# Moving work off ScalarE in an S5-scan and GeGLU kernel: one scaling for both parts of C, slab 3 normalised on VectorE, y of slab 1 a gate step later

## The chip, the cores and the metric

One core of a Trainium2 chip. The time is the device time of one execution in microseconds (us). Each kernel is timed in several executions beside executions of the kernel before on the same chip; one of them is profiled. The page of a profile gives the span, which is the time from the first to the last recorded instruction; executions take 2.1 to 3.3 us longer than their span. Engines: PE is TensorE (PEld its weight loads), ACT is ScalarE, DVE is VectorE, POOL is GpSimd, SP is SyncE, which issues most DMAs here. All executions told of were in the fast state.

## The reference

```python
xn = layernorm(x)                                   # x: 2048 tokens x 512
h[t] = Lam_bar * h[t-1] + xn[t] @ B_bar.T           # complex state, 512 wide
s = 2 * Re(h @ C.T) + xn * Dskip
g = silu((gelu(xn @ w_gate) * (xn @ w_up)) @ w_down)   # 512 -> 1376 -> 512
out = x + s * g
```

## The kernel before

Tokens are cut into four slabs (0 to 3) of 512. For each slab PE runs eleven gate steps (a gate and an up product of four matmuls each), the products u for the scan, and the down product f. The scan itself is on DVE: rotate (`pp`, `qq`, `Wt`), four scans (`Ft`), rotate back to `hst`. The output product y of a slab is put between the gate steps of the next one: eight matmuls add onto a seed (`z`, the skip term) that ACT has copied into the PSUM bank.

```python
U_BUFS = 3
Z_BUFS = 9
U0_AT = (5, 7)
Y_AT = {1: (9, 10, 11, 11), 2: (5, 6, 7, 8), 3: (2, 4, 6, 8)}   # gate steps that hold y of the slab before
XN_AT = {1: 1, 2: 3}                                            # gate steps that scale the slab after
...
def ffn(s, j, at):            # one gate step: PE products, two ACT evictions, every second step a DVE product
    g_ps, u_ps = gu_mm(s, j, 0), gu_mm(s, j, 1)
    ...
    ACT(out=gt[:fs, i, :], in_=g_ps[:fs, :], func=AF.Gelu_apprx_tanh)
    ACT(out=ub[:fs, i, :], in_=u_ps[:fs, :], func=AF.Copy)
    ...
    if j == NFT - 1:          # the last product, 96 rows
        dve(now() + lag, 0.36, lambda: TT(out=at[:fs, j, :], in0=gt[:fs, 0, :], in1=ub[:fs, 0, :], op=ALU.mult))
...
def y_seed(s, m):
    y_ps = psum.tile([P, D], FP32, name="y_ps", tag="ps")
    ACT(out=y_ps[:, :], in_=zs[s, m], func=AF.Copy)
...
def ln_out(s, m):             # xn = x * rstd - mean * rstd
    ACT(out=xn[:], in_=x_tok[:, s * M + m, :], func=AF.Identity, scale=rs[:, s, m : m + 1], bias=nb[:, s, m : m + 1])
    xn_out(s, m, xn)          # SP: DMA transpose of xn into xnT
...
            if s == 1:        # after slab 1's u products
                for m in (M - 2, M - 1):
                    epi(0, m, y_mm(0, m, hsts[0], y_pss[0, m]), g2s[0, m])   # ends in an output DMA on SP
            if s == 1:
                load_x(3)     # SP: x of slab 3
            for m in range(M):
                g2s[s, m] = down(s, m, ats[s])
                if s == 1:
                    ln_act(3, m)   # ACT: sums for the statistics of slab 3
```

`dve(ready, cost, f, late)` first lets older waiting DVE work out of a list as far as its estimated end allows, then emits `f`: the order on DVE is fixed when the kernel is built, by estimates. On the chip DVE keeps it: where it waits (0.66 us for y in a timeline below), the work behind waits too.

Of the kernel before, what the change touches and what calls it, by code (L numbers as in the profile page):

```python
# [10 lines left out]
AF = mybir.ActivationFunctionType  # L11
ALU = mybir.AluOpType
FP32 = mybir.dt.float32
# [6 lines left out]
def kernel(  # L20
# [17 lines left out]
    nc = tc.nc  # L38
    P = 128
    S = 2048  # L40
    D = 512
# [5 lines left out]
    NS = S // TS  # L47
    M = TS // P
    NFT = (F + P - 1) // P
# [7 lines left out]
    TSC = nc.vector.tensor_scalar  # L57
    STT = nc.vector.scalar_tensor_tensor
    ACT = nc.scalar.activation
# [5 lines left out]
    work = ctx.enter_context(tc.tile_pool(name="work", bufs=2))  # L65
# [5 lines left out]
    x_tok = consts.tile([P, NS * M, D], BF16, name="x_tok")  # L71
# [5 lines left out]
    C2 = consts.tile([P, 2, NPT, D], BF16, name="C2")  # L77
# [4 lines left out]
    CT = work.tile([P, 2, NPT, D], BF16, name="CT", tag="hst")  # L82
# [31 lines left out]
    for h in range(2):  # L114
        for ri, src in enumerate((A_B_re, A_B_im)):
            for pt in (h * H2, h * H2 + 1):
                nc.sync.dma_start_transpose(
                    out=BT[:, ri, :, pt * P : (pt + 1) * P], in_=src[pt * P : (pt + 1) * P, :]
# [27 lines left out]
    def small(name, w=NPT):  # L146
        return consts.tile([P, w], FP32, name=name)
# [9 lines left out]
    rs = consts.tile([P, NS, M], FP32, name="rs")  # L157

    def bn(s, m):
        nc.vector.bn_stats(out=st[:, s, m, :], in_=x_tok[:, s * M + m, :])  # L160
# [134 lines left out]
    cre, cim, ncre = small("cre"), small("cim"), small("ncre")  # L295
# [25 lines left out]
        GS(out=ncre[:], in0=cre[:], scalar1=-1.0, scalar2=None, op0=ALU.mult)  # L321

    def fold_c(pt):
        tA = work.tile([P, D], FP32, name="tA", tag="tt", bufs=3)
        tB = work.tile([P, D], FP32, name="tB", tag="tt", bufs=3)
        ACT(out=tA[:], in_=CT[:, 1, pt, :], func=AF.Copy, scale=cim[:, pt : pt + 1])
        ACT(out=tB[:], in_=CT[:, 0, pt, :], func=AF.Copy, scale=cim[:, pt : pt + 1])
        dve(now() + 0.8, 0.66, lambda: STT(
            out=C2[:, 0, pt, :], in0=CT[:, 0, pt, :], scalar=cre[:, pt : pt + 1], in1=tA[:],
            op0=ALU.mult, op1=ALU.subtract,  # L330
        ))
        dve(now() + 1.6, 0.66, lambda: STT(
            out=C2[:, 1, pt, :], in0=CT[:, 1, pt, :], scalar=ncre[:, pt : pt + 1], in1=tB[:],
            op0=ALU.mult, op1=ALU.subtract,
        ))

# [5 lines left out]
    def now():  # L342
        return clk["pe"]
# [9 lines left out]
    def flush(key):  # L353
        while any(w[3] == key for w in waiting):
            pop()

    def drain(t, late):
        while waiting and max(clk["dve"], waiting[0][0]) + waiting[0][1] <= t + late:
            pop()

    def dve(ready, cost, f, late=0.8):
        drain(ready, late)
        clk["dve"] = max(clk["dve"], ready) + cost
        f()

    def later(ready, cost, f, key=None):
        waiting.append((ready, cost, f, key))
# [1 line left out]

    ini = {}  # L370
    U_BUFS = 3
    Z_BUFS = 9
    U0_AT = (5, 7)
    Y_AT = {1: (9, 10, 11, 11), 2: (5, 6, 7, 8), 3: (2, 4, 6, 8)}
    XN_AT = {1: 1, 2: 3}

    def u_pair(s, h):
        cols = slice(s * TS, (s + 1) * TS)
# [126 lines left out]
# [3 lines that stand above are left out]
        y_pss[s, m] = y_ps  # L508
# [45 lines left out]
    nb = consts.tile([P, NS, M], FP32, name="nb")  # L554
    nm = consts.tile([P, NS, M], FP32, name="nm")
# [6 lines left out]
    def ln_small(s):  # L562
        total, var = sx[:, s, 0, :], sx[:, s, 1, :]

        def f():
            STT(out=mq[:, s, :], in0=total, scalar=-1.0 / (D * D), in1=total, op0=ALU.mult, op1=ALU.mult)
            TSC(out=nm[:, s, :], in0=total, scalar1=-1.0 / D, scalar2=None, op0=ALU.mult)
            STT(out=var, in0=var, scalar=1.0 / D, in1=mq[:, s, :], op0=ALU.mult, op1=ALU.add)
            TSC(out=var, in0=var, scalar1=EPS, scalar2=None, op0=ALU.add)

        dve(now() + 1.0, 0.3, f)
        nc.gpsimd.tensor_tensor(out=rs[:, s, :], in0=var, in1=mhalf[:], op=ALU.pow)
        nc.gpsimd.tensor_tensor(out=nb[:, s, :], in0=nm[:, s, :], in1=rs[:, s, :], op=ALU.mult)


    zs, y_pss = {}, {}
# [1 line left out]
    def skip(s, m, xn):  # L578
        if s == 0:

            z = x_tok[:, (NS - 1) * M + m, :]
        else:
            z = work.tile([P, D], BF16, name="z", tag="z", bufs=Z_BUFS)[:]
        zs[s, m] = z
        later(0.0, 0.36, lambda: TT(out=z, in0=xn[:], in1=Db[:], op=ALU.mult), ("z", s, m))

    def ln_out(s, m):
        flush(("z", s - 1, m))
        xn = work.tile([P, D], BF16, name="xn", tag="xn", bufs=4)
        ACT(out=xn[:], in_=x_tok[:, s * M + m, :], func=AF.Identity, scale=rs[:, s, m : m + 1], bias=nb[:, s, m : m + 1])  # L590
        xn_out(s, m, xn)

    def xn_out(s, m, xn):
        c0 = s * TS + m * P
        nc.sync.dma_start_transpose(out=xnT[:, :, c0 : c0 + P], in_=xn[:])
        if s > 1:
            skip(s, m, xn)


# [14 lines left out]
    def ln_vector_small(x):  # L614
        G.tensor_scalar(out=vx[:, x, :], in0=mv[:, x, :, 1], scalar1=EPS, scalar2=None, op0=ALU.add)
        G.tensor_tensor(out=rs[:, x, :], in0=vx[:, x, :], in1=mhalf[:], op=ALU.pow)
        G.tensor_tensor(out=nb[:, x, :], in0=mv[:, x, :, 0], in1=rs[:, x, :], op=ALU.mult)
        G.tensor_scalar(out=nb[:, x, :], in0=nb[:, x, :], scalar1=-1.0, scalar2=None, op0=ALU.mult)
# [9 lines left out]
    later(11.2, 1.25, lambda: TT(out=v5(t1_[:]), in0=sa, in1=cB, op=ALU.mult))  # L628
    later(11.2, 1.25, lambda: TT(out=v5(t2_[:]), in0=ca, in1=sB, op=ALU.mult))
    later(11.2, 1.25, lambda: TT(out=sin_b[:], in0=t1_[:], in1=t2_[:], op=ALU.add))  # L630
    xs1 = {}

    def norm1(m):
        xs1[m] = norm0(m, 1)

    for s in range(NS):
        for j in range(NFT):
            if s > 0 and j in Y_AT[s]:
                y_seed(s - 1, Y_AT[s].index(j))
            ffn(s, j, ats[s])  # L640
            if s == 0:
                if j == 1:
                    coefficients()
                if j == NFT - 1:
                    flush("n")
                    ln_vector_small(2)
                if j == 8:
                    coefficients_end()
                if j == 2:
                    flush("n1")  # L650
                    ln_vector_small(1)
                    rs1_at = clk["dve"] + 2.4
                if j == 3:
                    for m in range(M):
                        flush(("z", 0, m))
                        dve(max(rs1_at, 0.0), 0.36, lambda m=m: norm1(m), 0.4)
                        xn_out(1, m, xs1[m])
                if j in U0_AT:
                    chain(0, U0_AT.index(j), u_pair(0, U0_AT.index(j)), hst0)
                if j == 5:  # L660
                    for m in range(M):
                        later(0.0, 0.72, lambda m=m: (bn(2, m), bn_end(2, m)), "n")
                    for m in range(M):
                        skip(1, m, xs1[m])
                    nc.sync.dma_start(
                        out=wd[:, 0 : NFT - 1, :],
                        in_=B_w_down[0 : (NFT - 1) * P, :].rearrange("(k p) d -> p k d", p=P),
                    )
                    nc.sync.dma_start(out=wd[:FL, NFT - 1, :], in_=B_w_down[(NFT - 1) * P : F, :])
                    load_c()  # L670
            else:
                if j in Y_AT[s]:
                    m = Y_AT[s].index(j)
                    epi(s - 1, m, y_mm(s - 1, m, hsts[s - 1], y_pss[s - 1, m]), g2s[s - 1, m])
                if s < NS - 1 and XN_AT[s] <= j < XN_AT[s] + M:
                    ln_out(s + 1, j - XN_AT[s])
        if s < NS - 1:
            hsts[s + 1] = work.tile([P, 2, NPT, TS], BF16, name="hst", tag="hst")
            ats[s + 1] = work.tile([P, NFT, TS], BF16, name="at", tag="at")
            for h in range(2):  # L680
                chain(s + 1, h, u_pair(s + 1, h), hsts[s + 1])
                if s == 1:
                    y_seed(0, M - 2 + h)
            if s == 1:
                for m in (M - 2, M - 1):
                    epi(0, m, y_mm(0, m, hsts[0], y_pss[0, m]), g2s[0, m])
            if s == 1:
                load_x(3)
            for m in range(M):
                g2s[s, m] = down(s, m, ats[s])  # L690
                if s == 0:
                    fold_c(m)
                if s == 1:
                    ln_act(3, m)
            if s == 1:
                ln_small(3)
    s = NS - 1
# [41 lines left out]
```

## Time and profile before

| | before |
|---|---|
| time, median of the first 3 executions | 184.47 us |
| span of the profiled execution | 181.3 us |
| busy: PE, DVE, ACT | 175.1, 160.5, 116.0 us |
| idle time of PE in the middle of the run | 0.96 us, once |

### The profile page before, as it was taken

The page shows a single profiled execution, that of the slowest core. Times are in us where ns is not written, and L with a number is a line of the kernel's source. Part 1 is how long each engine was busy: PE and PEld are TensorE (multiplying, and loading weights), DVE is VectorE, ACT ScalarE, POOL GpSimd, SP SyncE. Part 2 cuts the span into 40 slices and gives each one's busy share as a digit, 9 for nine tenths or more (in the row PEclk, how much of TensorE's full clock was granted, in tenths as well). Part 3 has the DMA queues.
Part 4 walks back from the last instruction along what each step waited for, and adds up shares of the span by engine and source line. Part 5 has one row for each costly group of instructions (what it writes and reads, how often), then busy time and mean ns, then how long its engine had stood idle before and what let it go on. Part 6 is the DMA issues. An engine that isn't in the chain of part 4 may idle for free.

```text
span 181.3 us, 2449 instructions
## 1 busy us (share of the span) xinstructions
PE 175.1 (97%) x858; PEld 82.8 (46%) x858; DVE 160.5 (89%) x252; ACT 116.0 (64%) x206; POOL 21.5 (12%) x50
## 2 busy tenths in 40 slices
PE   7899999999999999999999799999999999999992
PEld 2684444444444444444444344444444444444451
DVE  3889999998978999999969999999999899996063
ACT  3599667777799982781599974467429545574500
POOL 3794416004000000000004000000000000000000
PEclk9999999999999999999999999999999999999999
DMA  5999497950002300002300223100000000000011
GB/s 154 312 337 185 95 240 224 255 90 9 0 0 50 66 4 29 29 0 68 106 4 0 42 58 74 36 29 0 0 0 0 29 5 29 29 29 0 0 55 61
DMA packets 25643, 12.37 MB, mean 68 GB/s; under 512 B 15808, under 2 KB 25632, under 8 KB 25632
## 3 DMA queue, kind: packets, MB, share of 16 engines
q1 hardware_dynamic: 25456, 12.16, 27.6%
q8 instruction: 6, 0.10, 0.2%
q10 hardware_dynamic: 176, 0.07, 0.1%
q14 instruction: 5, 0.04, 0.1%
HBM read 6.46 MB, written 2.10 MB: 47 GB/s over the span
## 4 chain that ended last, share of the span: by engine, by line
PE 64%; DVE 17%; ACT 12%; DMA 3%; issue 2%; SPq 0%; DVEq 0%; ACTq 0%
PE f_ps L495 16%; PE up_ps L243 13%; PE g_ps L243 13%; PE u_ps L387 11%; PE y_ps L515 11%; DVE Ft L434 4%; DMA x_tok<-in_A_x_dram 3%; ACT gt L479 3%; ACT ub L480 2%; ACT junk L560 2%; DVE pp L404 2%; DVE qq L404 2%; DVE yg L528 2%; DVE hst L408 1%; ACT L479 1%
## 5 line engine op out<-in xcount | busy, mean ns | idle before, releaser
L243 PE MATMUL g_ps<-xnT,wg 128*128 128x512 bf16 (+3 forms) x200 | 45.9, 353 | 0.3 <-DVE xnT L203 0.2
L243 PE MATMUL up_ps<-xnT,wu 128*128 128x512 bf16 (+3 forms) x192 | 45.7, 361 | 0.0
L495 PE MATMUL f_ps<-wd,at 128*128 128x512 bf16 (+1 forms) x176 | 38.7, 379 | 0.0
L479 ACT ACTIVATE gt<-g_ps 128x512 bf16<-128x512 f32 (+1 forms) x44 | 27.0, 614 | 16.4 <-PE g_ps L243 16.3
L480 ACT ACTIVATE ub<-up_ps 128x512 bf16<-128x512 f32 (+1 forms) x44 | 27.1, 616 | 5.7 <-PE up_ps L243 5.5
L434 DVE TENSOR_TENSOR_SCAN Ft<-rho,it,Wt 128x512 bf16<-128x512 f32 x24 | 29.3, 1268 | 0.0
L515 PE MATMUL y_ps<-C,hst 128*128 128x512 bf16 x120 | 27.9, 379 | 1.0 <-ACT y_ps L507 1.0
L387 PE MATMUL u_ps<-xnT,BT 128*128 128x512 bf16 x128 | 28.4, 379 | 0.0
L243 PEld LDWEIGHTS <-wg 128*128 128x128 bf16 (+1 forms) x200 | 19.1, 100 | 19.5 <-issue 0.5
L243 PEld LDWEIGHTS <-wu 128*128 128x128 bf16 (+1 forms) x192 | 18.8, 100 | 19.2
L495 PEld LDWEIGHTS <-at 128*128 128x128 bf16 (+1 forms) x176 | 17.2, 98 | 20.8
L392 ACT ACTIVATE U<-u_ps 128x512 bf16<-128x512 f32 x32 | 19.1, 597 | 9.8 <-PE u_ps L387 9.7
L500 ACT ACTIVATE g<-f_ps 128x512 f32<-128x512 f32 x16 | 9.5, 593 | 16.2 <-PE f_ps L495 16.2
L387 PEld LDWEIGHTS <-BT 128*128 128x128 bf16 x128 | 12.5, 98 | 15.0
L515 PEld LDWEIGHTS <-hst 128*128 128x128 bf16 x120 | 11.7, 98 | 15.3 <-issue 1.2
L528 DVE TENSOR_TENSOR yg<-y_ps,g 128x512 bf16<-128x512 f32 x15 | 10.3, 685 | 8.1 <-PE y_ps L515 8.1
L488 DVE TENSOR_TENSOR at<-gt,ub 128x1024 bf16<-128x1024 bf16 x20 | 13.6, 680 | 0.5 <-ACT ub L480 0.4
L408 DVE TENSOR_TENSOR hst<-pp,qq 128x1024 bf16<-128x1024 bf16 x16 | 10.6, 689 | 0.3
L408 DVE TENSOR_TENSOR Wt<-pp,qq 128x1024 bf16<-128x1024 bf16 x16 | 10.4, 688 | 0.2
L404 DVE TENSOR_TENSOR pp<-U,cos_b 128x2048 bf16<-128x2048 bf16 x8 | 9.7, 1218 | 0.1
L404 DVE TENSOR_TENSOR pp<-Ft,cos_b 128x2048 bf16<-128x2048 bf16 x8 | 9.8, 1219 | 0.0
L404 DVE TENSOR_TENSOR qq<-Ft,sin_b 128x2048 bf16<-128x2048 bf16 x8 | 9.8, 1219 | 0.0
(108 smaller groups left out, 146.9 us busy)
## 6 DMA issues: line engine op xcount, KB each, us to landing
out_dram<-ot SPq DMA_DIRECT2D x15, 128.0 KB, 1.7
x_tok<-in_A_x_dram SPq DMA_DIRECT2D x3, 512.0 KB, 6.7
wd<-in_B_w_down_dram SPq DMA_DIRECT2D x1, 1280.0 KB
wg<-in_B_w_gate_dram SPq DMA_DIRECT2D x2, 256.0 KB, 3.7
wu<-in_B_w_up_dram SPq DMA_DIRECT2D x2, 256.0 KB
wg<-in_B_w_gate_dram SPq DMA_DIRECT2D x1, 512.0 KB, 6.5
wu<-in_B_w_up_dram SPq DMA_DIRECT2D x1, 512.0 KB
wg<-in_B_w_gate_dram SPq DMA_DIRECT2D x1, 352.0 KB
```

The costliest lines, as they stand in the source:

```text
L243: nc.tensor.matmul(ps[:fs, a:b], lhsT=w[:, kt, fsl], rhs=xnT[:, kt, s * TS + a : s * TS + b], start=(kt == 0), stop=(kt == KT - 1),)
L387: nc.tensor.matmul(u_ps[:, :], lhsT=BT[:, ri, kt, pt * P : (pt + 1) * P], rhs=xnT[:, kt, cols], start=(kt == 0), stop=(kt == KT - 1),)
L392: ACT(out=U[:, ri, q, :], in_=u_ps[:, :], func=AF.Copy)
L404: TT(out=box[key][:], in0=src()[:], in1=tab[:, hs, :].unsqueeze(1).to_broadcast(W), op=ALU.mult)
L408: return lambda: TT(out=dst()[i], in0=box["pp"][:, i, :, :], in1=box["qq"][:, 1 - i, :, :], op=op)
L434: nc.vector.tensor_tensor_scan(out=box["F"][:, ri, q, :], data0=rho[:, pt : pt + 1].to_broadcast([P, TS]), data1=box["W"][:, ri, q, :], in ...
L479: ACT(out=gt[:fs, i, :], in_=g_ps[:fs, :], func=AF.Gelu_apprx_tanh)
L480: ACT(out=ub[:fs, i, :], in_=u_ps[:fs, :], func=AF.Copy)
L488: dve(now() + lag, 0.63, lambda: TT(out=at[:, j - 1 : j + 1, :], in0=gt[:], in1=ub[:], op=ALU.mult))
L495: nc.tensor.matmul(f_ps[:, :], lhsT=at[:fs, k, m0 : m0 + P], rhs=wd[:fs, k, :], start=(k == 0), stop=(k == NFT - 1))
L515: nc.tensor.matmul(y_ps[:, :], lhsT=hst[:, j // NPT, j % NPT, m0 : m0 + P], rhs=C2[:, j // NPT, j % NPT, :], start=False, stop=(j == 2 * N ...
L528: TT(out=yg[:], in0=y_ps[:, :], in1=g2[:], op=ALU.mult)
```

## The change

Its intent is to take ACT out of PE's way: fewer instructions on ACT (four of the eight scalings of C and the four xn of slab 3 go), and y of slab 1 one gate step later, to give its seed time.

```diff
     def fold_c(pt):
-        tA = ...; tB = ...                            # two tiles, 3 buffers of 512
-        ACT(out=tA[:], in_=CT[:, 1, pt, :], func=AF.Copy, scale=cim[:, pt : pt + 1])
-        ACT(out=tB[:], in_=CT[:, 0, pt, :], func=AF.Copy, scale=cim[:, pt : pt + 1])
+        tc_ = ...                                     # one tile, 2 buffers of 1024
+        ACT(out=tc_[:], in_=CT[:, :, pt, :], func=AF.Copy, scale=cim[:, pt : pt + 1])
...
-    Z_BUFS = 9
+    Z_BUFS = 8
-    Y_AT = {..., 2: (5, 6, 7, 8), ...}
-    XN_AT = {1: 1, 2: 3}
+    Y_AT = {..., 2: (6, 7, 8, 9), ...}
+    XN_AT = {1: 1, 2: 6}
...
     def ln_out(s, m):
+        if s == NS - 1:
+            dve(now() + 0.5, 0.36, lambda: TSC(
+                out=xn[:], in0=x_tok[:, s * M + m, :], scalar1=nm[:, s, m : m + 1], scalar2=rs[:, s, m : m + 1],
+                op0=ALU.add, op1=ALU.mult,
+            ))
+            xs3[m] = xn
+        else:
             ACT(...)                                  # as before, slab 2 only
...
+                if s == 2 and j in (XN_AT[2], XN_AT[2] + 1):
+                    for m in (2 * (j - XN_AT[2]), 2 * (j - XN_AT[2]) + 1):
+                        ln_out(3, m)                  # two xn in each of two steps
+                if s == 2 and j == NFT - 1:
+                    for m in range(M): skip(3, m, xs3[m])
```

(Cut: one small POOL product that the new form of xn doesn't need, and the loop of the old form.)

More of the change, by code (lines that the diff above doesn't have):

```diff
@@ L323, in fold_c @@
     def fold_c(pt):
-        tA = work.tile([P, D], FP32, name="tA", tag="tt", bufs=3)
-        tB = work.tile([P, D], FP32, name="tB", tag="tt", bufs=3)
-        ACT(out=tA[:], in_=CT[:, 1, pt, :], func=AF.Copy, scale=cim[:, pt : pt + 1])
-        ACT(out=tB[:], in_=CT[:, 0, pt, :], func=AF.Copy, scale=cim[:, pt : pt + 1])
+        tc_ = work.tile([P, 2, D], FP32, name="tc_", tag="tt", bufs=2)
+        ACT(out=tc_[:], in_=CT[:, :, pt, :], func=AF.Copy, scale=cim[:, pt : pt + 1])
         dve(now() + 0.8, 0.66, lambda: STT(
-            out=C2[:, 0, pt, :], in0=CT[:, 0, pt, :], scalar=cre[:, pt : pt + 1], in1=tA[:],
+            out=C2[:, 0, pt, :], in0=CT[:, 0, pt, :], scalar=cre[:, pt : pt + 1], in1=tc_[:, 1, :],
             op0=ALU.mult, op1=ALU.subtract,
@@ L332, in fold_c @@
         dve(now() + 1.6, 0.66, lambda: STT(
-            out=C2[:, 1, pt, :], in0=CT[:, 1, pt, :], scalar=ncre[:, pt : pt + 1], in1=tB[:],
+            out=C2[:, 1, pt, :], in0=CT[:, 1, pt, :], scalar=ncre[:, pt : pt + 1], in1=tc_[:, 0, :],
             op0=ALU.mult, op1=ALU.subtract,
@@ L371 @@
     U_BUFS = 3
-    Z_BUFS = 9
+    Z_BUFS = 8
     U0_AT = (5, 7)
-    Y_AT = {1: (9, 10, 11, 11), 2: (5, 6, 7, 8), 3: (2, 4, 6, 8)}
-    XN_AT = {1: 1, 2: 3}
+    Y_AT = {1: (9, 10, 11, 11), 2: (6, 7, 8, 9), 3: (2, 4, 6, 8)}
+    XN_AT = {1: 1, 2: 6}
     def u_pair(s, h):
@@ L572, in ln_small @@
         nc.gpsimd.tensor_tensor(out=rs[:, s, :], in0=var, in1=mhalf[:], op=ALU.pow)
-        nc.gpsimd.tensor_tensor(out=nb[:, s, :], in0=nm[:, s, :], in1=rs[:, s, :], op=ALU.mult)
     zs, y_pss = {}, {}
@@ L589, in ln_out @@
         xn = work.tile([P, D], BF16, name="xn", tag="xn", bufs=4)
-        ACT(out=xn[:], in_=x_tok[:, s * M + m, :], func=AF.Identity, scale=rs[:, s, m : m + 1], bias=nb[:, s, m : m + 1])
+        if s == NS - 1:
[5 more added lines that the diff above has]
+        else:
+            ACT(
+                out=xn[:], in_=x_tok[:, s * M + m, :], func=AF.Identity,
+                scale=rs[:, s, m : m + 1], bias=nb[:, s, m : m + 1],
+            )
         xn_out(s, m, xn)
@@ L595, in xn_out @@
         nc.sync.dma_start_transpose(out=xnT[:, :, c0 : c0 + P], in_=xn[:])
-        if s > 1:
+        if s == 2:
             skip(s, m, xn)
@@ L630 @@
     later(11.2, 1.25, lambda: TT(out=sin_b[:], in0=t1_[:], in1=t2_[:], op=ALU.add))
-    xs1 = {}
+    xs1, xs3 = {}, {}
     def norm1(m):
@@ L674 @@
                     epi(s - 1, m, y_mm(s - 1, m, hsts[s - 1], y_pss[s - 1, m]), g2s[s - 1, m])
-                if s < NS - 1 and XN_AT[s] <= j < XN_AT[s] + M:
-                    ln_out(s + 1, j - XN_AT[s])
+                if s == 1 and XN_AT[1] <= j < XN_AT[1] + M:
+                    ln_out(2, j - XN_AT[1])
+                if s == 2 and j in (XN_AT[2], XN_AT[2] + 1):
+                    for m in (2 * (j - XN_AT[2]), 2 * (j - XN_AT[2]) + 1):
+                        ln_out(3, m)
+                if s == 2 and j == NFT - 1:
+                    for m in range(M):
+                        skip(3, m, xs3[m])
         if s < NS - 1:
```

## The prediction

The sum is -1.12 us (the seed wait) + 0.5 (what DVE takes back) = -0.6. Measured: 0.325 us for an xn on DVE, 0.85 ns for an element on ACT. The 0.2 us by which weights load ahead is that of the trace of before: the load for the last product starts at 163.07, its matmul at 163.29.

> **What bounds the kernel now.** I read the head of the page first, then the list of everything that waited, then the stretches of time, then the timeline of one engine at a time around each place where TensorE (PE) is idle. The page gives the span (181.3 us), then each engine's busy time, share and instructions:
>
> ```profile
> span 181.3 us, 2449 instructions
> PE 175.1 (97%) x858; PEld 82.8 (46%) x858; DVE 160.5 (89%) x252; ACT 116.0 (64%) x206; POOL 21.5 (12%) x50
> ```
>
> PE lacks only 6.2 us of the span. Nor is there slack inside its busy time: four 512-wide matmuls follow each other in 0.863 us (starts 100.42 and 101.29 in the timeline), 0.216 us each, and the granted clock is 1.00. The change removes no matmul, so only idle PE time can be won. The waits of PE after its start-up (waiter, releaser, us in total, times, longest) are three:
>
> ```profile
> PE y_ps L515 <- ACT y_ps L507: 1.0, 1, 1.0
> PE g_ps L243 <- DVE xnT L203: 0.2, 1, 0.2
> PE tp L181 <- DVE xn L171: 0.2, 1, 0.2
> ```
>
> The last two are in the first 7 us. The remainder is start (about 1.2 us before the first matmul, small gaps to 6 us) and tail (last matmul ends 177.7). The change reaches only the first wait. In the stretches (busy us of PE, PEld, DVE, ACT, POOL; clock; DMA share; GB/s) it is the one dent in the middle:
>
> ```profile
> 75.00:90.00 15.00, 15.00 (x71) 6.79 (x70) 14.79 (x21) 8.03 (x16) 0.00 (x0) 1.00 0.16 52
> 90.00:105.00 15.00, 14.04 (x67) 6.24 (x65) 13.11 (x25) 14.88 (x32) 2.09 (x2) 1.00 0.09 19
> 105.00:120.00 15.00, 15.00 (x71) 7.03 (x70) 14.79 (x25) 8.19 (x15) 0.00 (x0) 1.00 0.20 55
> ```
>
> There ACT is full (14.88 of 15), elsewhere it idles. DVE is nearly full everywhere: that is the second thing to keep in mind. Timelines (start, us, instruction) of ACT and then of PE at the dent:
>
> ```profile
> 100.18 0.87 ACT L590 ACTIVATE xn<-x_tok,nb,rs 128x512 bf16<-128x512 bf16 x1
> 100.89 0.66 ACT L479 ACTIVATE gt<-g_ps 128x512 bf16<-128x512 f32 x1
> 101.36 0.67 ACT L480 ACTIVATE ub<-up_ps 128x512 bf16<-128x512 f32 x1
> 101.84 0.89 ACT L590 ACTIVATE xn<-x_tok,nb,rs 128x512 bf16<-128x512 bf16 x1
> 102.55 0.68 ACT L507 ACTIVATE y_ps<-z 128x512 f32<-128x512 bf16 x1
> ```
>
> ```profile
> 101.29 1.03 PE L243 MATMUL up_ps<-xnT,wu 128*128 128x512 bf16 x4
> 103.27 1.89 PE L515 MATMUL y_ps<-C,hst 128*128 128x512 bf16 x8 [0.96 <-ACT y_ps L507]
> ```
>
> The y matmuls of slab 1 add onto a seed that ACT writes into their bank. At gate step 5 of slab 2 ACT is still behind (it spent 88.0 to 95.0 on the statistics of slab 3), with two xn in front of the seed. The seed ends at 103.23; PE starts 0.04 later. PE lost more than the idle 0.96: the y matmuls would have started one group pitch after 101.29, at 102.15, so the stall costs 103.27 - 102.15 = 1.12 us.
>
> [...] 447 ns for xn on DVE (L171) and 419 for z (L585). I take the starts: four xn take 20.15 to 21.45, 0.325 us each. [...] Here 256 more elements cost 596 - 378 = 218 ns (L507 against L705), 0.85 ns each.
>
> **The change part by part.**
>
> One scaling for both parts of C: 8 ACT instructions become 4. Today tA and tB take 0.61 + 0.71 = 1.32 us (pitch, then last duration). One of 1024 wide should take 0.71 + 512 x 0.85 ns = 1.15 (estimate). ACT saves 4 x 0.17 = 0.7 us, three of the four times before a wait for PE, so nothing carries over. But DVE's first fold now waits for 1.15 instead of 0.71: +0.44 us. The last fold (50.91) leads to the product at 54.90 and scans to 57.84, before DVE's 0.40 idle for ub at 58.24. With +0.43 it comes to 58.27. So the idle absorbs it, and y of slab 0 (PE at 66.74, its hst ready at 66.52) moves by some 0.03: nothing on PE.
>
> Slab 3 scaled on DVE: ACT loses 4 xn of 0.71 us pitch, 2.8 us, just in the stretch where it is late. DVE gains 4 x 0.325 = 1.30 us and POOL loses one product nobody waits for.
>
> y of slab 1 at steps 6 to 9 instead of 5 to 8: a step is 1.73 us of PE. Without the stall PE reaches y at 102.15 + 1.73 = 103.88. The seed: without xn, ACT catches up with PE at step 5, whose up matmuls end by 102.3. Its copy starts at 102.37, the seed at 102.87 (pitch 0.50) and ends at 103.47: 0.4 early. Stall gone, **-1.12 us**. By the same count xn off ACT is enough by itself (with y left at step 5 the seed could start at about 101.15), whereas the later step alone is not (the seed would come after the third xn, at about 104.2, and PE would still lose some 0.9).
>
> Now what DVE does with its 1.30 us. Its queue runs from 95.06 to 166.2 with one idle gap, 0.53 at 142.34, so extra work there comes out later. The limit is the end of slab 3: the down matmuls need the last product (96 rows) at their eleventh matmul:
>
> ```profile
> 161.04 1.28 DVE L434 TENSOR_TENSOR_SCAN Ft<-rho,it,Wt 128x512 bf16<-128x512 f32 x1
> 162.24 0.40 DVE L486 TENSOR_TENSOR at<-gt,ub 96x512 bf16<-96x512 bf16 x1
> ```
>
> ```profile
> 161.13 9.67 PE L495 MATMUL f_ps<-wd,at 128*128 128x512 bf16 x44
> ```
>
> Today it is ready at 162.64 and its weights load about 0.2 before 161.13 + 10 x 0.216 = 163.29, near 163.08: 0.44 us spare. The instruction order of the changed kernel, which I compared, has only three of the last four scans before this product, not all four. So the product ends at 162.64 + 1.30 (xn) - 1.20 (scan) - 0.53 (the gap closes) + 0.2 (one y result, due 156.8, is now awaited) = 162.4. PE, 1.12 earlier, wants it at 161.96. So DVE takes back about **+0.5 us** (0 to 0.8, as this is a difference of large sums).
>
> Two more checks. hst of slab 3: four xn later, gap closed, to 167.25; y of slab 3 wants it at 169.5 or later, so it is hidden. xnT of slab 3: the second pair of xn comes after the second y result (109.1), about 112.1; two transposes issue at 112.6 and 113.8 (1.19 us each), landing 2.4 after issue, 116.2; u wants them at 117.7. Hidden, with 1.5 us spare against today's 5.7 (last issue 110.70, landed 113.1, wanted 118.8).
>
> Sum: -1.12 + 0.5 = -0.6 us of span, 181.3 to 180.7. Measured runs lie 3 us above the span; 184.47 - 0.6 = **183.8**.
>
> **The rivals.** (a) DVE takes nothing back: the order favours the last product by one scan, and DVE has had 0.44 spare. -1.12 makes 183.35. Against it: the xn time and PE's lead both eat into that 0.44. (b) DVE becomes the bound in slabs 2 and 3: the 1.30 us come out on PE in full and more, at a y bank released late or at the transposes. Then 184.5 to 185. For it: 14.8 of 15 us busy. Against: y banks return eight tiles later, over a microsecond after their release by my walk, and the transposes have 1.5 spare. (c) The longer scaling delays y of slab 0: its hst has only 0.2 us before PE wants it. If the 1024-wide instruction takes 1.4 rather than 1.15, up to 0.25 us is lost, making 184.05. (d) A reader of the ACT total would expect 2.8 + 0.7 = 3.5 us, 181 us; the share of PE forbids it, as ACT idles 65 us.
>
> **Range and chances.** 183.35 (a) and the sum 183.8 are the likely ends of the mechanism; the runs before scatter by 0.37 us[...]. Range 183.1 to 184.6. Faster by over 2% would need 180.8, more than all the idle PE time in reach: 1%. Slower by over 2% needs 3.7 us of new stall: 1%. Within 2%: 98%.
>
> **What would show it.** In the changed profile: no PE wait for the seed (L507's successor) and PE full from 90 to 160; y of slab 1 near 103.9; ACT at about 111.5 us busy (116.0 - 4 x 0.86 - 1.1); the scaling at 1.1 to 1.2 us; a short wait (0.2 to 0.7) of PE or its weight load for the 96-row product near 162; last matmul near 177. Wrong would be: PE waits at u of slab 3 (transposes), at y of slab 0 or 3 (hst), or a seed stall at a later step; or no wait at 162 at all, which is rival (a).

## The result

| | before | after |
|---|---|---|
| time, median of 6 executions | 184.57 us | 183.36 us |
| lowest to highest | 184.30 to 185.32 | 183.13 to 183.79 |
| span of the profiled execution | 181.3 | 181.0 |
| busy PE, DVE, ACT | 175.1, 160.5, 116.0 | 174.4, 162.0, 112.4 |

The ratio is 0.9933 (95% interval 0.9912 to 0.9954). A ratio is the mean time of the fast executions of one kernel over that of the other's of the same rounds, so not quite the ratio of the medians above.

The head of the page of after. Its PE busy time is a little too small, as 16 of the 858 matmul records are missing:

```profile
span 181.0 us, 2421 instructions
PE 174.4 (96%) x842; PEld 82.9 (46%) x858; DVE 162.0 (89%) x256; ACT 112.4 (62%) x198; POOL 21.7 (12%) x49
```

PE's waits in after (waiter, releaser, us in total, times, longest):

```profile
PE w_ps L153 <- DVE halfpi L126: 1.2, 1, 1.2
PE f_ps L493 <- DVE at L484: 0.6, 1, 0.6
PE tp L181 <- DVE xn L171: 0.2, 1, 0.2
PE g_ps L243 <- DVE xnT L203: 0.2, 1, 0.2
```

The wait for the seed is gone. In its place stands a wait of the down product f for the last product `at`. The stretches (columns as in the prediction) show the same: the dent at 90 to 105 has closed, and there is a new one at 150 to 165, where before PE was full (15.00 of 15).

```profile
90.00:105.00 15.00, 14.95 (x70) 6.80 (x70) 12.50 (x24) 14.75 (x34) 1.87 (x1) 1.00 0.00 1
150.00:165.00 15.00, 14.30 (x66) 6.57 (x67) 14.83 (x20) 7.65 (x12) 0.00 (x0) 1.00 0.08 26
```

The timelines of ACT and of PE where the seed was late:

```profile
102.45 0.60 ACT L478 ACTIVATE ub<-up_ps 128x512 bf16<-128x512 f32 x1
102.94 0.60 ACT L505 ACTIVATE y_ps<-z 128x512 f32<-128x512 bf16 x1
```

```profile
103.11 1.03 PE L243 MATMUL up_ps<-xnT,wu 128*128 128x512 bf16 x4
103.98 1.89 PE L513 MATMUL y_ps<-C,hst 128*128 128x512 bf16 x8
```

The seed ends at 103.54, and y starts one group pitch (0.87, the distance from the start of one group of four matmuls to the next) after 103.11: nothing lost. The timelines of DVE and of PE at the end of slab 3:

```profile
161.38 1.28 DVE L432 TENSOR_TENSOR_SCAN Ft<-rho,it,Wt 128x512 bf16<-128x512 f32 x1
162.57 0.40 DVE L484 TENSOR_TENSOR at<-gt,ub 96x512 bf16<-96x512 bf16 x1
```

```profile
160.11 2.32 PE L493 MATMUL f_ps<-wd,at 128*128 128x512 bf16 x10
163.02 7.53 PE L493 MATMUL f_ps<-wd,at 96*128 96x512 bf16 x33 [0.59 <-DVE at L484]
```

Ten matmuls of f run, the eleventh needs the 96 rows. It would have started at 160.11 + 10 x 0.216 = 162.27 and starts at 163.02, 0.05 after the product's end: 0.75 us lost.

To compare profiles I use one measure throughout: **lost** time of PE, in pitch. At the seed and at u it is the start of y (or u) less the start of the group before and 0.863; at the last product it is the time from the start of f to the start of y of slab 3, less 44 x 0.216 = 9.51. It counts more than the idle time that the profile prints, because a matmul's recorded end overlaps the next (a group of four is printed as 1.03 us where the next group starts after 0.86).

### The profile page after: what moved, and what is told of

It is laid out like the page before. It is cut to its first block, busy times and chain, and to the rows that moved or that the text cites. A ratio compares the mean times of both kernels' runs of the same rounds, so it can differ in the third digit from the quotient of the medians.

```text
span 181.0 us, 2421 instructions
## 1 busy us (share of the span) xinstructions
PE 174.4 (96%) x842; PEld 82.9 (46%) x858; DVE 162.0 (89%) x256; ACT 112.4 (62%) x198; POOL 21.7 (12%) x49
## 4 chain that ended last, share of the span: by engine, by line
DVE 44%; PE 42%; issue 5%; ACT 4%; DMA 3%; another core or an unknown queue 0%; SPq 0%; DVEq 0%; ACTq 0%
DVE Ft L432 12%; PE up_ps L243 10%; PE g_ps L243 10%; PE f_ps L493 9%; PE u_ps L385 8%; DVE qq L402 6%; DVE yg L526 5%; DVE pp L402 4%; PE y_ps L513 4%; DVE hst L406 4%; DMA x_tok<-in_A_x_dram 3%; DVE at L486 3%; DVE ot L527 3%; DVE Wt L406 3%; ACT junk L558 2%
## 5 line engine op out<-in xcount | busy, mean ns | idle before, releaser
L243 PE MATMUL g_ps<-xnT,wg 128*128 128x512 bf16 (+3 forms) x196 | 45.3, 353 | 0.5 <-DVE xnT L203 0.2
L243 PE MATMUL up_ps<-xnT,wu 128*128 128x512 bf16 (+3 forms) x188 | 45.2, 361 | 0.2
L402 DVE TENSOR_TENSOR qq<-U,sin_b 128x2048 bf16<-128x2048 bf16 x8 | 9.7, 1218 | 0.0
```

The costliest lines, as they stand in the source:

```text
L243: nc.tensor.matmul(ps[:fs, a:b], lhsT=w[:, kt, fsl], rhs=xnT[:, kt, s * TS + a : s * TS + b], start=(kt == 0), stop=(kt == KT - 1),)
L402: TT(out=box[key][:], in0=src()[:], in1=tab[:, hs, :].unsqueeze(1).to_broadcast(W), op=ALU.mult)
```

## The experiments

All twelve kernels computed the right result. Three calls of four kernels, each call on one chip with 11 executions of the kernel before beside it (medians 184.13, 184.25, 184.45 us; mean spans 181.77, 181.78, 181.72). Times are medians of 6 executions, one of them profiled.

| kernel | time | ratio to before | mean span | lost at seed | at u | at last product |
|---|---|---|---|---|---|---|
| before (first profile) | 184.57 | 1 | - | 1.12 | 0 | 0 |
| after (first profile) | 183.36 | 0.9933 | 181.23 | 0.01 | 0 | 0.77 |
| step alone | 184.48 | 1.0039 | 182.30 | 1.14 | 0 | 0.01 |
| scaling alone | 184.03 | 1.0000 | 181.73 | 1.15 | 0.01 | 0 |
| xn alone | 184.26 | 1.0005 | 181.67 | 0.01 | 0.40 | 0.27 |
| after, product first | 182.87 | 0.9943 | 180.62 | 0 | 0 | 0 |
| before, early load | 183.30 | 0.9956 | 180.97 | 0.32 | 0 | 0 |
| after, early load | 183.14 | 0.9943 | 180.88 | 0.01 | 0 | 0.27 |
| after again | 182.97 | 0.9935 | 180.77 | 0 | 0.01 | 0.27 |
| xn alone, sooner | 182.71 | 0.9928 | 180.55 | 0 | 0 | 0.01 |
| after, xn sooner | 182.93 | 0.9928 | 180.67 | 0 | 0 | 0.05 |
| after, xn later | 185.37 | 1.0059 | 183.13 | 0 | 2.11 | 0 |
| xn alone, sooner, early load | 182.70 | 0.9908 | 180.57 | 0 | 0.01 | 0.01 |
| xn alone, product first | 183.99 | 0.9967 | 181.35 | 0 | 1.10 | 0 |

### Each part of the change by itself

**The step alone.**

```diff
-    Y_AT = {..., 2: (5, 6, 7, 8), ...}      # before
+    Y_AT = {..., 2: (6, 7, 8, 9), ...}
```

> The kernel before with only y of slab 1 moved to gate steps 6 to 9 of slab 2; slab 3 is still scaled on ScalarE. My theory: the seed still follows the third xn of slab 3 in ScalarE's queue, so PE still waits about 0.9 us for it (0.5 to 1.6), and the time stays within 0.4 us of before (0.1 to 0.3 us faster). Rival 'the later step is what helped': the wait is gone and the run is about 1.1 us faster than before.

ACT and PE of its profile:

```profile
104.17 0.90 ACT L590 ACTIVATE xn<-x_tok,nb,rs 128x512 bf16<-128x512 bf16 x1
104.87 0.69 ACT L507 ACTIVATE y_ps<-z 128x512 f32<-128x512 bf16 x1
```

```profile
103.61 1.03 PE L243 MATMUL up_ps<-xnT,wu 128*128 128x512 bf16 x4
105.61 1.89 PE L515 MATMUL y_ps<-C,hst 128*128 128x512 bf16 x8 [0.98 <-ACT y_ps L507]
```

The seed stands directly behind the third xn, and PE waits as long as before. The rival falls. The small gain that I expected did not come: the executions were even 0.39% slower (one span of 183.4 among them), though the profile loses what before loses. The execution of 183.4 shows a mean granted clock of 0.991; only two others are that low, both of 'after, xn later', and each of the three is 1.0 us or more longer than the rest of its kernel. Why the others of this run were longer (182.3 and 182.4 at a clock of 1.00) is open.

**The scaling alone.** With 9 z buffers this did not fit in SBUF (its build stops with 113.25 kB per partition wanted by the work pool and 112.31 left), which is what the 8 in the change is for.

```diff
     # before, with fold_c of the change
-    Z_BUFS = 9
+    Z_BUFS = 8
```

> The kernel before with only the one 1024-wide scaling for both parts of C (and 8 instead of 9 z buffers, without which it does not fit in SBUF). My theory: ScalarE saves 4 x 0.17 = 0.7 us of busy time, of which PE sees nothing: the seed wait stays at 1 us or more, the time is within 0.2 us of before. Rival 'fewer ScalarE instructions are worth their time': 0.7 us faster.

Ratio 1.0000: PE sees nothing of it, as expected. The instruction itself, in after's timeline:

```profile
43.12 1.14 ACT L325 ACTIVATE tc__648<-CT,cim 128x1024 f32<-128x1024 bf16 x1
```

It takes 1.14 us in place of 1.32, and ACT then waits 0.75 us for PE.

**The xn alone.**

```diff
     # the change, with these parts put back as before
-    tc_ ... (one scaling)
+    tA, tB ... (two scalings, as before)
-    Y_AT = {..., 2: (6, 7, 8, 9), ...}
+    Y_AT = {..., 2: (5, 6, 7, 8), ...}
```

> The kernel before with only slab 3 scaled on VectorE (two xn at gate steps 6 and 7, its skip products at the last step); y of slab 1 stays at steps 5 to 8, C is scaled in two instructions. My theory: the seed is no longer behind xn; PE waits 0 to 0.4 us for it (0.4 if the load of slab 3 of x lands as late as in the profile of after), and waits 0.5 to 0.8 us for the last product of slab 3, as in after. Time within 0.3 us of after, 0.8 to 1.2 us faster than before. Rival 'the step is needed': the seed wait stays near 1 us and the run is as slow as before.

The seed is in time, as expected, but the run is no faster than before, which I had not expected. Its profile shows something new at u of slab 3:

```profile
116.84 1.03 PE L243 MATMUL up_ps<-xnT,wu 128*96 128x512 bf16 x4
118.10 7.07 PE L387 MATMUL u_ps<-xnT,BT 128*128 128x512 bf16 x31 [0.23 <-DMA xnT<-xn]
```

u waits for the transposes of xn. The profiled execution was the fastest of its six (span 180.8, the others 181.5 to 182.1), so the profile shows less of the loss than the others had. Two losses are candidates: the transposes (0.40) and the last product (0.27).

### Which of the two: the last product or the transposes

**xn alone, with the last product one scan sooner.**

```diff
     # in the last gate step, on top of 'xn alone'
-    dve(now() + lag, 0.36, lambda: TT(out=at[...], ...))
+    dve(now() + lag, 0.36, lambda: TT(out=at[...], ...), -1.2 if s == NS - 1 else 0.8)   # 'late'
```

> Slab 3 scaled on VectorE alone (xn at steps 6 and 7, y at 5 to 8), with the last product one scan earlier. The run without that had spans of 181.5 to 182.1 us when timed and lost 0.27 us at the last product and 0.40 at u in its profile of 180.8. My theory: the transposes are its main loss, so the product's place wins at most 0.3 us: spans of 181.2 to 181.8, ratio to before 0.997 to 1.0, a PE wait at u of slab 3 in the profile. Rival 'the last product was its loss': spans of 180.6 to 180.8 and a ratio of 0.993, as with the changed kernel with the product first.

```profile
117.43 1.03 PE L243 MATMUL up_ps<-xnT,wu 128*96 128x512 bf16 x4
119.39 6.85 PE L387 MATMUL u_ps<-xnT,BT 128*128 128x512 bf16 x30 [0.93 <-DMA xnT<-xn]
```

The last product loses nothing now, and u still 1.10 us. The spans fall in two groups: 180.6 and 180.7 in two executions, 181.3 to 181.9 in four. The profiled one is of the longer group, and its transposes of slab 3 took 3.1 to 3.5 us from issue to landing; what lengthened them is open (in the profile of 'xn alone' they took 2.4 to 3.5). So in the longer group the transposes are the main loss, as my theory said. The two shorter executions met the figure of the rival (180.6 to 180.8); none of them was profiled.

**xn alone, xn a step sooner.**

```diff
     # on top of 'xn alone'
-    XN_AT = {1: 1, 2: 6}
+    XN_AT = {1: 1, 2: 5}
```

> Slab 3 scaled on VectorE alone, y at steps 5 to 8, as in the earlier run of that kind, but the xn at steps 5 and 6 instead of 6 and 7, so that in the queue of SyncE each pair of transposes stands one output DMA earlier. My theory: the earlier run was no faster than before because its transposes landed late at u of slab 3; sooner, they land in time, no PE wait at u, and the time is that of after, 0.8 to 1.2 us faster than before. Rival 'y at step 5 costs the time, not the transposes': as slow as the earlier run, i.e. as before.

No loss is left and the ratio is 0.9928, a little more than the 0.8 to 1.2 us expected. With y at its old steps and C scaled as before, moving xn is all that the change needs, if its transposes come soon enough. (This also moves scans behind the last product, so it isn't a clean test of the transposes; the next pair is.)

**After with xn sooner, and with xn later.** These two have the same DVE order at the end of slab 3 and differ only in when xn and its transposes come.

```diff
     # after
-    XN_AT = {1: 1, 2: 6}
+    XN_AT = {1: 1, 2: 5}      # sooner; in the other kernel 7, later
```

> The changed kernel with the four xn of slab 3 one gate step sooner on VectorE (steps 5 and 6). By the order of instructions the two pairs of transposes then stand before the first and the second output DMA of slab 1, and one scan fewer follows the last y of slab 2 before the last product. My theory: transposes land 2 us or more before u wants them, the last product is in time or at most 0.2 us late, no PE wait of over 0.2 us after the start; 0.1 to 0.5 us faster than after (ratio to before 0.990 to 0.993). Rival 'the 1.3 us of VectorE come out on PE somewhere': another PE wait appears and the time stays that of after.

> The changed kernel with the four xn one gate step later (steps 7 and 8); its VectorE order at the end of slab 3 is that of the run with xn sooner, so the two differ only in when xn and its transposes come. My theory: the last transpose is issued about 2.7 us later than in after (117.5), lands at about 120, and PE waits 1.5 to 3 us at u of slab 3; the run is 1 to 2.5 us slower than after, about as slow as before or slower. Rival 'transposes have room': no wait at u, time that of after.

Later costs 2.11 us at u:

```profile
117.19 1.03 PE L243 MATMUL up_ps<-xnT,wu 128*96 128x512 bf16 x4
120.16 6.20 PE L385 MATMUL u_ps<-xnT,BT 128*128 128x512 bf16 x27 [1.94 <-DMA xnT<-xn]
```

The mean spans differ by 183.13 - 180.67 = 2.5 us; without the two executions of 'later' at a clock of 0.991 (184.1 and 184.3) by 1.9. The times expected of the transposes held in both; that 'sooner' is faster than after is not shown (0.9928 against 0.9935). After itself sits on the edge between them, as its timelines of SP (DMA issues) and PE show:

```profile
112.95 0.53 SPq L530 DMA_DIRECT2D out_dram<-ot  x1
113.58 2.61 SPq L602 DMA_TRANSPOSE xnT<-xn  x2
```

```profile
117.79 7.07 PE L385 MATMUL u_ps<-xnT,BT 128*128 128x512 bf16 x31
```

The last transpose is issued at 115.0 and lands 2.6 later, at 117.6: 0.2 us before u wants it. In the queue of SP the pair stands behind an output DMA of y. That is what the later step of y does for the change: with y at step 5 and xn at step 6 ('xn alone') one more output DMA goes first (two, at 106.94 to 110.68, before the pair at 110.78; in after one, at 109.93, before the pair at 110.36). On DVE one more y result and one more scan go first as well (the second pair of transposes is issued at 114.26 there, at 113.58 here); how much of the lateness is the queue's and how much DVE's was not separated.

### What DVE gives back at the last product

**After with the last product first.** The same edit of `late` as above, on after.

> The changed kernel with the last product of slab 3 (96 rows) put one scan earlier in VectorE's queue, directly after the product before it. My theory: the product is ready at about 161.8, before PE wants it at 162.1, so PE's wait of 0.6 us (0.75 us in pitch) in the down matmuls of slab 3 goes away, hst of slab 3 is still in time (about 167.9 against 169.6), and the run is 0.6 to 0.8 us faster than after, so 1.6 to 2.0 us faster than before. Rival 'VectorE is the bound of the tail': the wait only moves to y of slab 3 and the time stays that of after.

The loss at the last product is gone and moves nowhere: y of slab 3 starts at 160.30 + 9.51 = 169.81. The wait that the rival forecast at y did not come, though the time stayed near that of after. The gain expected (0.6 to 0.8) was too large: mean spans are 180.62 against 180.77 of after again, on another chip, and the ratios (0.9943, 0.9935) don't tell the two apart; it had one execution of 184.0, whose span was 180.7.

**After with the earlier load.** The load of slab 3 of x is issued two output DMAs sooner, right after the last seed that reads its space.

```diff
             if s == 1:
+                load_x(3)
                 for m in (M - 2, M - 1):
                     epi(0, m, y_mm(0, m, hsts[0], y_pss[0, m]), g2s[0, m])
-            if s == 1:
-                load_x(3)
```

> The changed kernel with the same earlier load. My theory: VectorE's long run of work from the slab 3 statistics on starts about 1 us earlier, so the last product of slab 3 is ready in time, the transposes of slab 3 land about 1 us before u wants them, and the run is 0.6 to 1.2 us faster than after. Rival 'the give-back comes from the xn on VectorE themselves, whatever its start': PE still waits over 0.4 us at the last product.

> The changed kernel unaltered, as the control on this chip: 0.9 to 1.5 us faster than before by the first measurement (0.993), and a profile of another execution: PE waits for the last product of slab 3 again (0.4 to 0.9 us); it waits for the transposes at u of slab 3 in some executions (0 to 0.4 us), as only 0.2 us were spare in the first profile.

No gain (0.9943 against 0.9935): my expectation failed. The rival's wait of over 0.4 us did not come either, and after again lost less than I expected: 0.27 in both. The DVE timeline of the early load shows why (a line of 0.42 us, `ot`, is cut after the first):

```profile
157.34 0.69 DVE L526 TENSOR_TENSOR yg<-y_ps,g 128x512 bf16<-128x512 f32 x1 [0.66 <-PE y_ps L513]
158.41 2.45 DVE L432 TENSOR_TENSOR_SCAN Ft<-rho,it,Wt 128x512 bf16<-128x512 f32 x2
160.78 0.67 DVE L486 TENSOR_TENSOR at<-gt,ub 128x1024 bf16<-128x1024 bf16 x1
161.36 1.28 DVE L432 TENSOR_TENSOR_SCAN Ft<-rho,it,Wt 128x512 bf16<-128x512 f32 x1
162.55 0.40 DVE L484 TENSOR_TENSOR at<-gt,ub 96x512 bf16<-96x512 bf16 x1
```

DVE did come sooner, and then waited 0.66 us for the last y of slab 2. From the start of that y's epilogue (`yg`) to the end of the last product is a fixed 162.95 - 157.34 = 5.61 us of DVE work, with three scans in it. So 0.27 us are lost however early DVE is: 'xn alone', where DVE waited 0.24 us for that y, lost 0.27 too. Only another order takes them away, as in the runs above with the product first or xn sooner. Above that floor comes what DVE is late by. In after's first profile PE was 0.48 us further on than in after again (f starts at 160.11 and 160.59), but the statistics of slab 3, which wait for the load, started at the same time (88.74 and 88.75; the load was issued at 84.81 and 85.27). So the product ended at the same time too (162.97 and 162.95), and the first lost 0.77, the second 0.27. Nobody waited for the transposes in after again.

### Was it the number of instructions on ACT?

**Before with the earlier load.** The same edit on the kernel before; all of ACT's instructions stay where they are.

> The kernel before, with the load of slab 3 of x issued two output DMAs earlier (after the last seed that reads its space, some 4.5 us sooner); nothing else. My theory: the root of the seed wait is that ScalarE's statistics of slab 3 wait for this load (2.6 us at 88.0), which makes ScalarE late. Its statistics then end about 1 us earlier, held by the last silu, so the seed wait shrinks from 1.0 to about 0.1 us and the run is 0.9 to 1.2 us faster than before, with all twelve instructions still on ScalarE. Rival 'ScalarE simply has too many instructions in that stretch': the wait stays above 0.7 us and the time is that of before.

0.9956, two thirds of the change's gain (0.44% of 0.67%) for one moved line. ACT's first statistic, in before and with the early load:

```profile
88.02 0.63 ACT L560 ACTIVATE junk<-x_tok 128x512 bf16<-128x512 bf16 x1 [2.56 <-DMA x_tok<-in_A_x_dram]
```

```profile
85.95 0.62 ACT L560 ACTIVATE junk<-x_tok 128x512 bf16<-128x512 bf16 x1
```

It now follows ACT's silu without a wait, and y starts 1.18 us after the start of the up products instead of 1.98:

```profile
101.89 1.03 PE L243 MATMUL up_ps<-xnT,wu 128*128 128x512 bf16 x4
103.07 1.89 PE L515 MATMUL y_ps<-C,hst 128*128 128x512 bf16 x8
```

So most of ACT's lateness (0.80 of 1.12 us) came of statistics that waited 2.6 us for a load. The wait shrank to 0.32 us in pitch, not to 0.1: a little less than expected, and enough for the rival to fall. The 0.32 that are left go only in the kernels without xn on ACT in front of the seed.

### The best of them

**xn alone, xn sooner, with the earlier load.**

> The best candidate: slab 3 scaled on VectorE at steps 5 and 6, y of slab 1 at steps 5 to 8, C scaled in two instructions as before, and the earlier load of slab 3. The run without the earlier load had no PE wait left after the start in its profile. My theory: nothing is left to win there, so the same time as that run (ratio to before 0.992 to 0.994), only with more room for a late load. Rival 'the late load still costs in executions that were not profiled': 0.3 us or more faster than that run.

```profile
PE w_ps L153 <- DVE halfpi L126: 1.2, 1, 1.2
PE tp L181 <- DVE xn L171: 0.3, 1, 0.3
PE g_ps L243 <- DVE xnT L203: 0.2, 1, 0.2
```

PE's waits are those of the start alone. The ratio is 0.9908 (0.9890 to 0.9927), the lowest of all: 182.70 us against 184.45 of before in the same rounds. Part of that is the executions of before in this call, which took 2.67 us more than their spans in the mean, against 2.28 and 2.37 in the other calls. Its mean span (180.57) is that of the run without the earlier load (180.55), so whether the earlier load adds anything here stays open, and so does whether either beats after (180.77 in after again). Between start and tail only matmul pitch remains in its profile.

## Why the prediction was right or wrong

The time, 183.36 us against 183.8 predicted, lay in the range, and the class (within 2%) was the one given 98%.

- **PE is the bound, and only the seed wait can be won: right.** The reader of ACT's total (rival d) would have been wrong by 2.4 us; the scaling alone, 0.7 us of ACT, is worth nothing.
- **The seed wait costs 1.12 and goes: right in size.** Lost 1.12, 1.14 and 1.15 us in the three profiles that have the wait untouched, 0.01 or less in every kernel with xn on DVE.
- **"By the same count xn off ACT is enough by itself": wrong as put.** It is enough for the seed, but the run won nothing until xn came a step sooner. The step of the argument that failed is the second of the "two more checks".
- **That check, the transposes, "1.5 us spare": the result (hidden) right in after's profiles, the size wrong.** The last transpose was issued at 115.0 and not 113.8, as DVE's second pair of xn came 0.7 us later (the statistics began 0.72 later, at the load), an output DMA stood before it, and the issues follow each other in 1.4 us rather than 1.2; and it took 2.6 to land rather than 2.4. Spare were 0.2 us. In neighbouring orders PE lost 0.4 to 2.1 us here.
- **The later step alone leaves about 0.9: right, a little low** (1.14 in pitch, 0.98 idle).
- **DVE gives back 0.5 at the last product: right in mechanism, its size partly luck.** It was 0.77 and 0.27 in two executions. The working had all terms for DVE (xn, one scan fewer, the gap that closes, one y result awaited), but did not see that the last of them makes a floor of 0.27 which no earlier start of DVE removes. The mis-sized term is PE's: it was said to want the product 0.2 us before the eleventh matmul, for the weights. In after's first profile, where they waited, the product ended at 162.97, and the weight load and the matmul are both recorded at 163.02, 0.05 later. Without these 0.2 the working gives about 0.3. The first profile's further 0.5 came of the load, which the working had left out.
- **Rival (a), DVE takes nothing back, 183.35 us:** the time measured, 183.36, is its figure by luck, as both profiles of after show a loss at the last product.
- **The scaling 1.15 us: right** (1.14). hst of y of slab 0 did not delay PE (rival c falls). ACT busy 112.4, not 111.5: busy time counts overlapped instructions once (in before an xn of 0.89 us starts at 101.84 and the seed 0.71 later, at 102.55), so the pitches are the right unit, 4 x 0.71 + 4 x 0.18 = 3.6 us less.
- **The sum, -0.6, was too small; measured -1.2.** By after again: -1.15 (seed) + 0.27 = -0.88 of span, against 181.78 - 180.77 = 1.0 measured in mean spans; 0.2 more lies between span and time (2.37 us in before, 2.18 in after again, in the same rounds). So of the missing 0.6 about 0.23 is the give-back, 0.2 the time outside the span, and the rest is open. The two profiles first compared, 181.3 and 181.0, make the gain look like 0.3: the one before was of a short execution, apart from the six timed ones (183.56 us, where their median is 184.57). The same mix made the prediction say that runs lie 3 us above the span; that execution lay 2.3 above its own.

## What to carry to other kernels

When one engine is 97% busy, count the places where it waits, not the instructions of the others; then ask why the engine it waits for was late. Here a load stood behind two output DMAs in SP's queue (issued at 84.70 us in before, at 80.75 with the earlier load), and moving that one line was worth two thirds as much as the whole change. When work moves to another engine, follow it to all its consumers, through the DMA queue as well: a consumer with 0.2 us to spare, as u had here, becomes the bound when its input comes a little later (xn one step later cost 2.1 us), and by how much can differ between executions of one kernel ('xn alone' had spans of 180.8 to 182.1).

Two profiles, one of each kernel, mislead about a change of 1 us: the spans of the kernel before went from 181.3 to 182.1 us, and PE reached y of slab 0 at 66.84 us in the first profile of after and at 67.31 in the second.

Of single instructions the runs show this. A transpose of xn (128x512 bf16) took 1.19 to 1.34 us of SP's queue in the first profiles of before and after, and from issue to landing 2.4 to 4.1 us; those of slab 3 took 2.4 to 3.5 in the profiles read for it. The new xn on DVE took 406 ns in after and z, a product of the same shape, 418 (medians).
